# A decode attention kernel: transposes, scores and value product in rounds of 1024 rows, with the evacuation waits moved

## The chip, the cores and the metric

One core of a Trainium2 chip. The calls ran on several chips; the kernel before took a median of 1342.2 to 1343.5 us in every call. The metric is the device time of one execution, in microseconds (us), as the median of several timed runs. Every run told of below was in the fast state; the slow state that programs can fall into did not occur in a run that is used here. A "ratio" is the mean time of one kernel's fast runs over the mean of the other's fast runs of the same rounds, so it is not quite the ratio of the medians that are quoted.

## The reference, cut to what matters

```python
B, Sq, D = 2, 1, 448;  Hq, Hkv, Sk, Dh = 16, 8, 32768, 256      # bf16
q = (x @ wq)                                    # 16 heads, 2 per K/V head
scores = einsum("bhqd,bhkd->bhqk", q, k) * Dh ** -0.5
p = softmax(scores);  a = einsum("bhqk,bhkd->bhqd", p, v) @ wo
out = g * a + (1 - g) * mlp(x)                  # g: a sigmoid gate, small
```

One token a batch row reads all of a K and a V cache of 268 MB each. All else is small. So there are two long jobs: bring 547 MB in, and pass every row of K and V through TensorE.

## The kernel before

The work is cut into 16 groups (batch row × K/V head) of 4 tiles of 8192 rows each, and into units of 512 rows, 1024 in all. A K tile and a V tile are 4 MB each; they land in a ring of five slots. A unit takes three stages on TensorE:

- `T`: 8 transposes of 128x128 blocks of K into a PSUM bank, which ScalarE (even units) or VectorE (odd units) then evacuates to SBUF;
- `B`: scores, 8 matmuls with those blocks as weights (128 columns) and the two query heads of the group moving (2 columns);
- `C`: value product, 4 matmuls with the two heads' probabilities as weights (2 columns) and a row block of V moving (256 columns).

`B` runs 2 units behind `T` (`LB`), `C` 88 units behind (`DU`), because the softmax of a group has to be known first. The last group alone has another form of `C`: V as weights of 128 columns, the probabilities moving.

```python
NB, LB, NKT, NPB = 5, 2, 5, 3          # ring slots, lag of B, SBUF and PSUM buffers of K's transposes
DU = NT * NBL + NBL + NBL // 2         # 88

def T(U):
    wait_landed(E, d, bl)
    if U >= NPB:
        E.wait(evac_eng(U - NPB), ("E", U - NPB))       # bank free again
    for i in range(2 * BR): ... e.transpose(bank[...], kv[:, r, ...], ident_b)

def B(U):
    E.wait(evac_eng(U), ("E", U))                       # this unit evacuated
    ... 8 matmuls, weights buf[:, 128 columns], moving qT_sb (2 columns)

def C(v, bl):
    wait_landed(E, d, bl)
    ... 4 matmuls, weights pt[:, n, :] (2 columns), moving kv[:, r, :] (256 columns)

for U in range(NSTEPU):
    if U < UNITS: T(U)
    if 0 <= U - LB < UNITS: B(U - LB)
    # ... small products of the softmax chain (M1, M2, L, OT), cut ...
    if U >= DU: C((U - DU) // NBL, (U - DU) % NBL)
```

The SP queue issues the loads in the order of need; each waits until TensorE has released the slot.

## Time and profile before

| | before |
|---|---|
| time, median (3 runs) | 1342.33 us |
| span of the profiled run | 1339.0 us |
| TensorE matmul row busy | 98% |
| DMA over the span | 411 GB/s |

The prediction shows and reads the page's busy shares, its chain, the order of instructions and the waits. Three lines of the page (granted TensorE clock, busy share of the 16 DMA engines and GB/s, each in 40 slices) and the loads (count, KB each, us from issue to landing) complete it:

```profile
PEclk9799999999999999999999999999999999999997
DMA  9999999999999999999999999999999999999997
GB/s 394 435 424 431 423 412 420 416 409 417 411 415 413 412 416 410 417 408 409 410 419 412 405 418 410 420 407 414 411 407 417 416 411 413 406 415 416 412 403 301
...
ring<-in_A_k_cache_dram SPq DMA_DIRECT2D x63, 4096.0 KB, 14.6
ring<-in_A_v_cache_dram SPq DMA_DIRECT2D x63, 4096.0 KB, 15.3
```

The DMA row is at 9 up to the last slice, and yet the rate is 423 to 435 in slices 2 to 5 and some 405 to 420 later: an engine counts as busy while a packet is in flight, fast or slow, and from 300 to 1200 us a 32 KB packet took 1.26 us on average (median 1.21).

### The profile page before, as it was taken

What the parts mean: (1) busy time and instruction counts of PE and PEld (TensorE: products, weight loads), DVE (VectorE), ACT (ScalarE), POOL (GpSimd) and SP (SyncE); (2) the same over time, 40 slices, a digit from 0 to 9 for tenths busy, and PEclk for the clock granted to TensorE, in tenths of its full rate; (3) what the DMA queues carried; (4) which work ended last, traced back from release to release, by engine and by line L of the source; (5) the groups of instructions that cost most, each with busy time, mean ns of one, the idle gap of its engine ahead of it and who ended that gap; (6) DMA issues with size and microseconds to landing.
All of it is one profiled execution on the core that took longest, in us unless ns stands there. A gap on an engine that the chain in (4) does not pass through costs nothing.

```text
span 1339.0 us, 44891 instructions
## 1 busy us (share of the span) xinstructions
PE 1309.4 (98%) x21141; PEld 1017.9 (76%) x21141; DVE 387.2 (29%) x641; ACT 538.6 (40%) x597; POOL 1.5 (0%) x10
## 2 busy tenths in 40 slices
PE   4899999999999999999999999999999999999998
PEld 4887777777777777777777777777777777777776
DVE  2342322323223232322322223232232322323220
ACT  2464433434344443343434344343343434444330
POOL 0000000000000000000000000000000000000000
PEclk9799999999999999999999999999999999999997
DMA  9999999999999999999999999999999999999997
GB/s 394 435 424 431 423 412 420 416 409 417 411 415 413 412 416 410 417 408 409 410 419 412 405 418 410 420 407 414 411 407 417 416 411 413 406 415 416 412 403 301
DMA packets 22424, 550.30 MB, mean 411 GB/s; under 512 B 2392, under 2 KB 4576, under 8 KB 4704
## 3 DMA queue, kind: packets, MB, share of 16 engines
q1 hardware_dynamic: 22084, 547.43, 97.8%
q8 instruction: 165, 2.70, 0.7%
q14 instruction: 19, 0.16, 0.0%
q10 hardware_dynamic: 156, 0.01, 0.0%
HBM read 547.43 MB, written 0.00 MB: 409 GB/s over the span
## 4 chain that ended last, share of the span: by engine, by line
PE 96%; DMA 3%; SPq 1%; issue 0%; ACT 0%; DVE 0%
PE psT L374 41%; PE ps_o L448 38%; PE ps_s L393 13%; DMA ring<-in_A_k_cache_dram 3%; PE ps_o L453 1%; PE psT L462 1%; PE ps_m L426 1%; SPq L314 0%; PE ps_m L409 0%; PE ps_m L404 0%; PE ps_o L348 0%; PE ps_o L352 0%; PE ps_o L360 0%; SPq L301 0%; PE ps_m L415 0%
## 5 line engine op out<-in xcount | busy, mean ns | idle before, releaser
L507 ACT COPY KT<-psT 128x1024 bf16<-128x1024 bf16 x512 | 518.3, 1012 | 744.6 <-PE psT L374 744.6
L374 PE MATMUL psT<-ident_b,ring 128*128 128x128 bf16 x8192 | 640.1, 221 | 11.3 <-DMA ring<-in_A_k_cache_dram 9.7
L374 PEld LDWEIGHTS psT<-ident_b,ring 128*128 128x128 bf16 x8192 | 465.3, 98 | 222.6 <-issue 203.1
L509 DVE COPY KT<-psT 128x1024 bf16<-128x1024 bf16 x512 | 354.2, 692 | 901.7 <-PE psT L374 901.6
L448 PE MATMUL ps_o<-ring,PT 128*2 128x256 bf16 x3840 | 570.8, 272 | 0.0
L393 PE MATMUL ps_s<-qT_sb,KT 128*128 128x2 bf16 x8192 | 351.3, 164 | 1.1 <-issue 0.9
L393 PEld LDWEIGHTS ps_s<-qT_sb,KT 128*128 128x128 bf16 x8192 | 313.3, 96 | 1.9 <-issue 1.5
L448 PEld LDWEIGHTS ps_o<-ring,PT 128*2 128x2 bf16 x3840 | 244.6, 82 | 69.0
L537 ACT ACTIVATE PT<-ps_s,negm 128x256 bf16<-128x256 f32 x32 | 16.5, 545 | 0.5
L453 PE MATMUL ps_o<-PT,ring 128*128 128x2 bf16 x512 | 13.8, 164 | 2.1 <-issue 2.1
L453 PEld LDWEIGHTS ps_o<-PT,ring 128*128 128x128 bf16 x512 | 13.5, 100 | 2.8 <-issue 2.8
L340 PE MATMUL ps_m<-xT,ring 128*128 128x2 bf16 x128 | 3.5, 165 | 9.4 <-DMA ring<-in_A_wq_dram 9.4
L598 DVE TENSOR_REDUCE mx<-ps_s 128x2 f32<-128x512 f32 x16 | 10.9, 682 | 1.1 <-PE ps_s L393 1.1
L340 PEld LDWEIGHTS ps_m<-xT,ring 128*128 128x128 bf16 x128 | 3.5, 104 | 9.5 <-issue 9.5
L462 PE MATMUL psT<-ring,attnT 128*2 128x448 bf16 x32 | 9.8, 481 | 0.3 <-DVE attnT L625 0.3
L426 PE MATMUL ps_m<-ident_f,o_sb 2*128 2x2 f32 x60 | 9.4, 258 | 0.3 <-DVE o_sb L621 0.3
L621 DVE TENSOR_SCALAR o_sb<-ps_o,rl 2x256 f32<-2x256 f32 x15 | 7.1, 472 | 6.7 <-PE ps_o L448 6.5
L426 PEld LDWEIGHTS ps_m<-ident_f,o_sb 2*128 2x128 f32 x60 | 8.1, 191 | 0.6 <-DVE o_sb L621 0.4
L462 PEld LDWEIGHTS psT<-ring,attnT 128*2 128x2 bf16 x32 | 3.2, 105 | 5.7 <-issue 4.1
L625 DVE TENSOR_TENSOR attnT<-ps_o,rl 128x2 bf16<-128x2 f32 x2 | 0.2, 159 | 23.3 <-PE ps_o L453 23.3
L404 PE MATMUL ps_m<-ident_f,mx 128*2 128x128 f32 x32 | 6.1, 272 | 0.0
L409 PE MATMUL ps_m<-diag,ones_f 2*128 2x2 f32 x32 | 6.1, 256 | 0.0
(54 smaller groups left out, 61.9 us busy)
## 6 DMA issues: line engine op xcount, KB each, us to landing
ring<-in_A_k_cache_dram SPq DMA_DIRECT2D x63, 4096.0 KB, 14.6
ring<-in_A_v_cache_dram SPq DMA_DIRECT2D x63, 4096.0 KB, 15.3
ring<-in_A_k_cache_dram SPq DMA_DIRECT2D x4, 1024.0 KB, 16.5
ring<-in_A_v_cache_dram SPq DMA_DIRECT2D x4, 1024.0 KB, 17.3
ring<-in_A_wo_dram SPq DMA_DIRECT2D x1, 3584.0 KB, 14.6
ring<-in_A_wq_dram SPq DMA_DIRECT2D x1, 3072.0 KB, 10.2
ring<-in_B_w_dram SPq DMA_DIRECT2D x1, 1568.0 KB, 35.2
ring<-in_B_w_dram SPq DMA_DIRECT2D x1, 1344.0 KB, 30.7
```

What stands on the lines that cost most here:

```text
L340: E.ins(lambda e, w=w, xk=xk, kc=kc, kvh=kvh, j=j, hh=hh: e.matmul(ps_qT[:, kvh, j, hh, :], w, xk, start=(kc == 0), stop=(kc == KC)), key= ...
L374: E.ins(lambda e, bank=bank, i=i, kv=kv, r=r, j=j: e.transpose(bank[:, i * P:(i + 1) * P], kv[:, r, j * P:(j + 1) * P], ident_b[:, :]), ke ...
L393: E.ins(lambda e, pss=pss, n=n, i=i, j=j, buf=buf, kvh=kvh, b=b: e.matmul(pss[:, n, :], buf[:, (2 * i + j) * P:(2 * i + j + 1) * P], qT_sb ...
L426: E.ins(lambda e, j=j: e.matmul(ps_m[:, C_OT + 2 * j:C_OT + 2 * j + 2], o_sb[g % 2][0:2, j:Dh:2], ident_f[0:2, 0:2], start=True, stop=True ...
L448: E.ins(lambda e, g=g, kv=kv, r=r, n=n, pt=pt: e.matmul(ps_o[g % 2][0:2, 0:Dh], pt[:, n, :], kv[:, r, :], start=(n == 0), stop=(n == NT * ...
L453: E.ins(lambda e, g=g, kv=kv, r=r, n=n, j=j, pt=pt: e.matmul(ps_o[g % 2][:, 2 * j:2 * j + 2], kv[:, r, j:Dh:2], pt[:, n, :], start=(n == 0 ...
L462: E.ins(lambda e, c=c, kvh=kvh, hh=hh, j=j: e.matmul(ps_a, attnT[:, kvh, j, hh, :], wo_v[:, h, j * Dm:(j + 1) * Dm], start=(c == 0), stop= ...
L507: E.ins(lambda e: e.copy(buf[:, :], bank[:, :]), key=("E", U))
L509: E.ins(lambda e: e.tensor_copy(buf[:, :], bank[:, :]), key=("E", U))
L537: E.ins(lambda e, hh=hh: e.activation(PT[g % 2][:, :, hh], ps_s[g % 2][:, :, hh], ACTF.Exp, bias=negm[g % 2][:, hh:hh + 1], scale=SCALE, a ...
L598: E.ins(lambda e: e.tensor_reduce(mx[g % 2][:, :], ps_s[g % 2].rearrange("p n h -> p h n"), AX.X, ALU.max), key=("MX", g))
L621: E.ins(lambda e: e.tensor_scalar(o_sb[g % 2][:, :], ps_o[g % 2][0:2, 0:Dh], rl[g % 2][0:2, 0:1], None, op0=ALU.mult), key=("OS", g))
```

## The change

The intent: fewer borders between the stages, and no wait at the head of the transposes and scores, so that their weights could be loaded ahead.

```diff
@@ T @@
-                if U >= NPB:
+                if NPB <= U <= DU + 1:
                     E.wait(evac_eng(U - NPB), ("E", U - NPB))
@@ B @@
-                E.wait(evac_eng(U), ("E", U))
+                if U + LB <= DU + 1:
+                    E.wait(evac_eng(U), ("E", U))
@@ C @@
+            def wait_units(U):
+                for V in (U, U + 1):
+                    if V < UNITS:
+                        E.wait(evac_eng(V - NPB), ("E", V - NPB))
+                for V in (U - LB, U + 1 - LB):
+                    if V < UNITS:
+                        E.wait(evac_eng(V), ("E", V))
+
-            def C(v, bl):
+            def C(v, bl, ahead=None):
 ...
+                    if ahead is not None and i == 2:
+                        wait_units(ahead)
@@ main loop @@
-            for U in range(NSTEPU):
-                if U < UNITS:
-                    T(U)
-                if 0 <= U - LB < UNITS:
-                    B(U - LB)
 ...
-                if U >= DU:
-                    C((U - DU) // NBL, (U - DU) % NBL)
+            for U0 in range(0, NSTEPU, 2):
+                pair = (U0, U0 + 1)
+                for U in pair:
+                    if U < UNITS:
+                        T(U)
+                for U in pair:
+                    if 0 <= U - LB < UNITS:
+                        B(U - LB)
 ... (the small products, for U in pair)
+                for U in pair:
+                    if U >= DU:
+                        C((U - DU) // NBL, (U - DU) % NBL, U0 + 2 if U % 2 else None)
```

## The prediction

> **What bounds the kernel now.** I read the page of the run before first (busy shares, slices, the chain that ended last), then the waits of the engines and of the DMA queue, then the instructions in order of time, then the stretches of the span with their DMA rate.
>
> The page says TensorE:
>
> ```profile
> PE 1309.4 (98%) x21141; PEld 1017.9 (76%) x21141; DVE 387.2 (29%) x641; ACT 538.6 (40%) x597; POOL 1.5 (0%) x10
> ...
> PE psT L374 41%; PE ps_o L448 38%; PE ps_s L393 13%; DMA ring<-in_A_k_cache_dram 3%; PE ps_o L453 1%; PE psT L462 1%; PE ps_m L426 1%; SPq L314 0%; PE ps_m L409 0%; PE ps_m L404 0%; PE ps_o L348 0%; PE ps_o L352 0%; PE ps_o L360 0%; SPq L301 0%; PE ps_m L415 0%
> ```
>
> The chain is TensorE for 96% of the span: transposes of K (L374), value product (L448), scores (L393). The queue's own waits agree: every load of a ring slot waited for TensorE to release the slot, hardly ever the reverse.
>
> ```profile
> SPq L314 <- PE ps_o L448: 618.2, 59, 11.0
> SPq L314 <- PE ps_s L393: 609.3, 64, 17.2
> ```
>
> But a busy matmul row does not mean that work flows. The instructions in order of time, one unit of 512 rows in mid-kernel (columns: start us, length us, engine, line):
>
> ```profile
> 600.43 0.27 PE L448 MATMUL ps_o<-ring,PT 128*2 128x256 bf16 x1
> 600.63 0.45 PEld L374 LDWEIGHTS psT<-ident_b,ring 128*128 128x128 bf16 x8 [0.22 <-issue]
> 600.64 0.62 PE L374 MATMUL psT<-ident_b,ring 128*128 128x128 bf16 x8
> ...
> 601.10 0.34 PE L393 MATMUL ps_s<-qT_sb,KT 128*128 128x2 bf16 x8
> ...
> 601.37 0.60 PE L448 MATMUL ps_o<-ring,PT 128*2 128x256 bf16 x4
> 601.89 0.45 PEld L374 LDWEIGHTS psT<-ident_b,ring 128*128 128x128 bf16 x8 [0.22 <-issue]
> 601.90 0.62 PE L374 MATMUL psT<-ident_b,ring 128*128 128x128 bf16 x8
> ```
>
> First matmul to first matmul: transposes 0.46 us, scores 0.27, value product 0.53: 1.26 us a unit. Now the same transposes and scores before the value product has begun:
>
> ```profile
> 64.22 0.61 PE L374 MATMUL psT<-ident_b,ring 128*128 128x128 bf16 x8
> ...
> 64.67 0.34 PE L393 MATMUL ps_s<-qT_sb,KT 128*128 128x2 bf16 x8
> ...
> 64.87 0.61 PE L374 MATMUL psT<-ident_b,ring 128*128 128x128 bf16 x8
> ```
>
> There they take 0.45 and 0.20. And four value matmuls alone need (0.60 − 0.27)/3 = 0.11 each, 0.43 together. So a unit holds 0.45 + 0.20 + 0.43 = 1.08 us of work and 0.18 us of switching: about 0.07 going into the value product and 0.11 going out of it (0.10 before the weight load of L374 and 0.01 in its first matmul).
>
> **Is that switch a wait on a semaphore, or a cost of the switch itself?** The first transpose carries a wait on an evacuation. Two observations say that the wait is not the cause. In the stretch at 64 us the same transposes carry the same waits, and their weight loads follow the last score matmul without a gap. And late in the kernel a 128-column weight load follows a 2-column product with no semaphore to wait for (the final projection, L462, then the last value product, L453):
>
> ```profile
> 1321.28 1.30 PE L462 MATMUL psT<-ring,attnT 128*2 128x448 bf16 x6
> ...
> 1322.51 0.57 PEld L453 LDWEIGHTS ps_o<-PT,ring 128*128 128x128 bf16 x20 [0.39 <-issue]
> ```
>
> Its last matmul starts at 1322.23 and streams for 0.19 us (448 columns, by the spacing of its neighbours), to 1322.42; the load comes 0.09 us later, the same gap as at 600.54 to 600.63. So the 0.18 us is the price of going from 128-column weights to 2-column weights and back.
>
> **What the Trainium skill says.** "TensorE: Matmul & The Clock Gate", step-by-step section: the engine pulls weight loads ahead of matmuls in flight. The trace agrees within a stage and from transposes to scores, and differs at the border to and from the value product, where nothing is pulled ahead. The same page, section on weight-path modes: fast weight load is on only for weights of 128 columns that are not fp32. L374 and L393 have 128, L448 has 2, so the border is one between two kinds of load; the trace shows the gap, not the mode. "DMA: Bandwidth & Descriptors", Specifications: a fabric ceiling of 435 GB/s. The trace, in the stretch at the start where TensorE waits for K, comes close to it with 428:
>
> ```profile
> 50.00:160.00 110.00, 107.78 (x1903) 91.52 (x1904) 38.55 (x66) 52.72 (x57) 0.00 (x0) 0.94 1.00 428
> 160.00:300.00 140.00, 140.00 (x2209) 107.33 (x2206) 40.57 (x66) 57.56 (x65) 0.00 (x0) 1.00 1.00 414
> 300.00:1290.00 990.00, 990.00 (x15621) 759.90 (x15620) 289.38 (x472) 406.02 (x448) 0.00 (x0) 1.00 0.99 413
> ```
>
> The last three columns are granted clock, DMA busy share, GB/s. After 160 us TensorE alone sets the rate at 413. The busy share is near 1 in both, so it does not show the reserve; the rate does.
>
> **The change part by part.** (1) Two units a round: TTBBCC instead of TBCTBC. Arithmetic, bytes and evacuations are unchanged; one of two switches into and out of the value product goes: 0.18 us a pair. All three stages run together for units 88 to 1023, 936 units or 468 pairs: 468 × 0.18 = 84 us of TensorE time. Before unit 88 and after 1023 there is little to save. (2) The waits leave the transposes and scores; four stand in the value product, ahead of the third matmul of its second unit. At most three become instructions of their own on the sequencer, which runs about a unit ahead; I give them nothing. The last evacuation must be there in time. From the round's start: second transposes are all issued at 0.86 us; the vector copy starts 0.26 us after such an issue (601.04 to 601.30 for the scalar one) and takes 0.69, so it ends near 1.8; the scalar copy, for the first unit, runs 0.66 to 1.68. The waiting matmul is due at 0.90 + 0.40 + 0.09 + 6 × 0.108 = 2.03, its weight load one matmul earlier, 1.92. So the wait is over some 0.1 us before it is needed. (3) Once a group of 64 units the softmax chain on ScalarE (two exponentials of 0.55 + 0.18 us) may delay an evacuation: 0.1 to 0.2 us × 16, under 3 us.
>
> Thus TensorE's unit falls from 1.26 to about 1.17 us. A group now takes 81.77 us (the transposes of the output recur in the chain at 185.73, 267.50, 349.27); 64 × 1.26 = 80.64, so 1.13 goes to the group's small products. TensorE alone would come to 1342 − 84 = 1258.
>
> **But the transfers can't follow.** A K and a V tile are 8.39 MB for 16 units: 16 × 1.17 + 1.13/4 = 19.0 us, 441 GB/s. More than the 428 measured and the skill's 435. So the bound moves to DMA. When TensorE waits for data, two of five ring slots are in use and three are on order, so the queue stays deep, as in the 428 stretch. Floor, as an estimate: the page's 550.30 MB at 428 GB/s are 1286 us; 2 us before the first packets; 7.6 us from the last landing (TensorE resumes at 1331.4) to the end at 1339.0; 3 us for the 16 engines not finishing together (in the 428 stretch the first and last completion of one load lie 3 to 5 us apart). Sum 1299 us of span. The timed median is 3.3 us above the profiled span: **1302 us**, 3.0% faster. Of 84 us about 40 arrive.
>
> **Rivals.** *TensorE keeps the bound, with a new stall in the value product:* if the wait ends late, each round loses it. The margin is only 0.1 us, and TensorE has 0.3 us a tile to give (9.5 against DMA's 9.8), four rounds, so 0.07 us a round, before it is again the slower. A stall of 0.10 us a round leaves 468 × 0.08 = 37 us, 1305; one of 0.14 leaves 19 us, 1323; one over 0.18 is a loss. For it: the close margin. Against it: neither copy has other work in most rounds. *The gap belongs to the wait after all:* then moving the waits would save all switches, 1258 without DMA, but DMA still gives 1302. *No reserve in DMA:* busy share 0.99 already; if saturated transfers average 10.05 us for 4 MB rather than 9.8, about 1325, within 2%. For it: loads of 4 MB landed 10.2 us apart through the steady part, and some packets take longer than usual. Against it: from 50 to 120 us seven loads landed 9.93 us apart, and mid-kernel issue to landing stays near 14.5 us without growing, so the queue runs almost dry there. *Slower* needs a stall of over 0.24 us a round, twice what the margin could be wrong by.
>
> **Range and chances.** DMA at 428 to 432 with little skew gives 1290; a partial stall or a rate of 421 gives 1320. The 2% line is 1315.5. Faster 0.82, within 0.15, slower 0.03.
>
> **What would show it.** Rounds of 2.34 us where data are there: 16 transposes, 16 scores, 8 value matmuls, each with one gap of 0.09. GB/s in the middle rising from 413 to about 426; the wait of transposes or value product for the ring's loads appearing by some 30 to 45 us in total; issue to landing rising from 14.6 to over 20 us; hardly any wait of L448 for an evacuation. It is wrong if TensorE still shows no wait for loads, if idle time stands within the eight value matmuls, or if the rate stays at 413 with deep queues.

## The result, and the profile after

| | before | after |
|---|---|---|
| time, median (4 runs each, same rounds) | 1342.24 us | 1312.27 us |
| ratio of the fast runs | | 0.9779 (0.9762 to 0.9796) |
| span of the profiled run | 1339.0 us | 1310.5 us |
| DMA over the span | 411 GB/s | 420 GB/s |

Faster by 2.2%. The page of the changed kernel, the lines for the engines, the rate and the chain that ended last:

```profile
PE 1232.0 (94%) x21141; PEld 1028.0 (78%) x21141; DVE 388.7 (30%) x641; ACT 538.6 (41%) x597; POOL 1.5 (0%) x10
...
GB/s 394 435 421 423 428 430 429 430 429 428 426 428 430 429 430 428 426 428 429 429 429 416 425 426 427 425 427 422 421 419 423 422 428 418 430 419 421 429 346 295
...
PE 51%; DMA 47%; SPq 1%; issue 0%; DVE 0%
```

The chain was TensorE for 96% before; now DMA holds 47% of it. The rate stays near its early level up to the last two slices. The loads now wait in a deep queue:

```profile
ring<-in_A_k_cache_dram SPq DMA_DIRECT2D x63, 4096.0 KB, 29.8
ring<-in_A_v_cache_dram SPq DMA_DIRECT2D x63, 4096.0 KB, 31.4
```

From issue to landing is twice what it was: with a load landing about every 10 us, about three 4 MB loads are on order. And TensorE now waits for them (columns of the waits: us in total, times, longest):

```profile
PEld psT L374 <- issue: 100.4, 433, 1.7
PEld psT L374 <- DMA ring<-in_A_k_cache_dram: 54.1, 41, 5.7
PE psT L374 <- DMA ring<-in_A_k_cache_dram: 42.3, 34, 5.7
...
PE ps_o L464 <- DMA ring<-in_A_v_cache_dram: 13.9, 2, 13.7
```

"issue" ahead of the transposes' weight loads, the border out of the value product, came 898 times and 203 us before; it is now 433 times and 100 us: half. One round where the data are there:

```profile
601.25 0.90 PEld L374 LDWEIGHTS psT<-ident_b,ring 128*128 128x128 bf16 x16 [0.23 <-issue]
601.25 1.07 PE L374 MATMUL psT<-ident_b,ring 128*128 128x128 bf16 x16
...
602.16 0.54 PE L394 MATMUL ps_s<-qT_sb,KT 128*128 128x2 bf16 x16
...
602.63 1.03 PE L459 MATMUL ps_o<-ring,PT 128*2 128x256 bf16 x8
...
603.59 0.90 PEld L374 LDWEIGHTS psT<-ident_b,ring 128*128 128x128 bf16 x16 [0.22 <-issue]
603.60 1.07 PE L374 MATMUL psT<-ident_b,ring 128*128 128x128 bf16 x16
```

2.35 us for two units instead of 2 × 1.26 = 2.52. The eight value matmuls take 0.97 us to the next transposes, 8 × 0.109 + 0.10: no stall among them, though the waits now stand there. The gap ahead of the transposes is as long as before, though these carry no wait any more.

### The profile page after: what moved, and what is told of

Its sections match the earlier page's. It is cut to its first block, busy times and chain, and to the rows that moved or that the text cites. A ratio compares the mean times of both kernels' runs of the same rounds, so it can differ in the third digit from the quotient of the medians.

```text
span 1310.5 us, 45768 instructions
## 1 busy us (share of the span) xinstructions
PE 1232.0 (94%) x21141; PEld 1028.0 (78%) x21141; DVE 388.7 (30%) x641; ACT 538.6 (41%) x597; POOL 1.5 (0%) x10
## 4 chain that ended last, share of the span: by engine, by line
PE 51%; DMA 47%; SPq 1%; issue 0%; DVE 0%
DMA ring<-in_A_k_cache_dram 45%; PE psT L374 22%; PE ps_o L459 19%; PE ps_s L394 8%; DMA ring<-in_A_v_cache_dram 3%; SPq L314 0%; PE ps_m L427 0%; PE ps_o L348 0%; SPq L301 0%; PE ps_m L410 0%; PE ps_m L405 0%; PE ps_o L352 0%; PE ps_o L360 0%; PE psT L473 0%; PE ps_o L464 0%
## 5 line engine op out<-in xcount | busy, mean ns | idle before, releaser
L374 PE MATMUL psT<-ident_b,ring 128*128 128x128 bf16 x8192 | 553.4, 221 | 45.8 <-DMA ring<-in_A_k_cache_dram 42.3
L459 PE MATMUL ps_o<-ring,PT 128*2 128x256 bf16 x3840 | 497.1, 273 | 0.2
L459 PEld LDWEIGHTS ps_o<-ring,PT 128*2 128x2 bf16 x3840 | 284.5, 83 | 84.6 <-issue 0.6
L394 PE MATMUL ps_s<-qT_sb,KT 128*128 128x2 bf16 x8192 | 278.4, 163 | 0.8 <-issue 0.8
L394 PEld LDWEIGHTS ps_s<-qT_sb,KT 128*128 128x128 bf16 x8192 | 259.6, 96 | 1.0 <-issue 1.0
L464 PE MATMUL ps_o<-PT,ring 128*128 128x2 bf16 x512 | 14.2, 164 | 16.4 <-DMA ring<-in_A_v_cache_dram 13.9
L464 PEld LDWEIGHTS ps_o<-PT,ring 128*128 128x128 bf16 x512 | 13.7, 100 | 17.1 <-DMA ring<-in_A_v_cache_dram 14.0
## 6 DMA issues: line engine op xcount, KB each, us to landing
ring<-in_A_k_cache_dram SPq DMA_DIRECT2D x63, 4096.0 KB, 29.8
ring<-in_A_wo_dram SPq DMA_DIRECT2D x1, 3584.0 KB, 29.8
```

Of the source, the lines that this page charges most:

```text
L374: E.ins(lambda e, bank=bank, i=i, kv=kv, r=r, j=j: e.transpose(bank[:, i * P:(i + 1) * P], kv[:, r, j * P:(j + 1) * P], ident_b[:, :]), ke ...
L394: E.ins(lambda e, pss=pss, n=n, i=i, j=j, buf=buf, kvh=kvh, b=b: e.matmul(pss[:, n, :], buf[:, (2 * i + j) * P:(2 * i + j + 1) * P], qT_sb ...
L459: E.ins(lambda e, g=g, kv=kv, r=r, n=n, pt=pt: e.matmul(ps_o[g % 2][0:2, 0:Dh], pt[:, n, :], kv[:, r, :], start=(n == 0), stop=(n == NT * ...
L464: E.ins(lambda e, g=g, kv=kv, r=r, n=n, j=j, pt=pt: e.matmul(ps_o[g % 2][:, 2 * j:2 * j + 2], kv[:, r, j:Dh:2], pt[:, n, :], start=(n == 0 ...
```

## The experiments

The theory after the result: (1) the border into and out of the value product costs 0.18 us, whatever waits stand there, and pairing saves one of two; (2) that would be worth 80 us, but the loads set the end. Left open by the result: the loads ended 14 us later than I had worked out. All runs of one call share the runs of the kernel before.

### 1. The rounds alone, and the waits alone

`e1_pairs_only` takes the changed kernel and puts the waits back:

```diff
-                if NPB <= U <= DU + 1:
+                if U >= NPB:
...
-                if U + LB <= DU + 1:
-                    E.wait(evac_eng(U), ("E", U))
+                E.wait(evac_eng(U), ("E", U))
...
-  C(..., U0 + 2 if U % 2 else None)
+  C(...)
```

> The rounds of two units, with the waits left at the head of the transposes and of the scores, as before. Theory (the gain is one switch a pair, and the loads are then the bound): same as the changed kernel, 1312 +/- 3 us, DMA about 420 GB/s over the span, the gap ahead of the transposes still 0.09 us, once a pair. Rival (the wait at the head keeps weights from being loaded ahead, so the moved waits are part of the gain): TensorE keeps more gaps and the time lies between, 1318 to 1335 us.

Measured: 1312.17 us, ratio to before 0.9773 (0.9759 to 0.9788), correct. The same as the whole change. Its timeline:

```profile
600.61 0.90 PEld L374 LDWEIGHTS psT<-ident_b,ring 128*128 128x128 bf16 x16 [0.23 <-issue]
```

`e2_waits_only` takes the kernel before, with units one by one, and moves the waits for the next unit ahead of the third value matmul:

```diff
+            def wait_unit(U):
+                if U < UNITS: E.wait(evac_eng(U - NPB), ("E", U - NPB))
+                if U - LB < UNITS: E.wait(evac_eng(U - LB), ("E", U - LB))
...
+                    if ahead is not None and i == 2: wait_unit(ahead)
...
-                    C((U - DU) // NBL, (U - DU) % NBL)
+                    C((U - DU) // NBL, (U - DU) % NBL, U + 1)
```

(with the waits in `T` and `B` dropped as in the change)

> The order of before (one unit a round), with the waits for the next unit's evacuations moved into the value product ahead of its third matmul. Theory (a done wait costs nothing, the gap belongs to the change between 2-column and 128-column weights): same as before, 1342 +/- 3 us, unit 1.26 us, gap ahead of the transposes still 0.09 us. Rival (the wait causes the gap): the gap of 0.09 to 0.10 us at the head of the transposes goes in 936 units, so TensorE is faster by up to 85 us and the time falls to the loads' floor, about 1312 us.

Measured: 1346.64 us, ratio 1.0028 (1.0017 to 1.0039), correct. In its timeline, the gap is there without a wait:

```profile
601.31 0.45 PEld L374 LDWEIGHTS psT<-ident_b,ring 128*128 128x128 bf16 x8 [0.23 <-issue]
```

What follows: all of the gain is the order; the moved waits give nothing in either order, and alone cost about 4 us. (In the order of rounds both kernels end at the loads' floor, so their times alone could not show it. Before the loads bind, the first three groups take 76.12 us in both.) In the instruction records the first transpose starts 205 ns after the last value matmul in all three (before, with the waits moved, and after), so the gap is not the wait's. Where the 4 us arise I did not settle: seven of 13 groups still take 81.77 to 81.79 us, the others up to 0.9 us more, which is 2.9 us in all; the moved waits also bring 877 more instructions (45768 against 44891).

### 2. Less work for TensorE

`e3_before_light` and `e3_after_light` stream half of V's columns in the value product. They compute a wrong result on purpose, and load everything.

```diff
-  ps_o[g % 2][0:2, 0:Dh], pt[:, n, :], kv[:, r, :],
+  ps_o[g % 2][0:2, 0:(Dh if n == 0 else P)], pt[:, n, :], kv[:, r, 0:(Dh if n == 0 else P)],
```

> Wrong result on purpose. The order and the waits of before, as many instructions, but value matmuls stream 128 columns of V instead of 256 (the very first of a group still 256). TensorE's unit falls by about 4 x 0.054 = 0.21 us to 1.05 us, all bytes are still loaded. Theory (the changed kernel stands at the floor of the loads): about the time of the changed kernel, 1312 +/- 4 us, though the order is that of before and TensorE has 130 us less to do. Rival (the changed kernel is still bound by TensorE): well below 1312, down to 1270 us.

> Wrong result on purpose. The changed kernel with value matmuls of 128 columns instead of 256, same number of instructions and bytes. Theory (floor of the loads): 1312 +/- 3 us, no gain, TensorE's waits for loads grow by about 100 to 190 us in total. Rival (TensorE or its stalls still bound part of the run): 1270 to 1300 us.

Measured: 1312.17 and 1312.62 us, ratios 0.9774 (0.9757 to 0.979) and 0.9779 (0.9764 to 0.9793); both outputs wrong, as meant. From 300 to 1200 us (the last three columns are granted clock, DMA share, GB/s), first the order of before, then that of after:

```profile
300.00:1200.00 900.00, 820.05 (x14602) 708.64 (x14601) 269.79 (x443) 379.00 (x422) 0.00 (x0) 0.93 1.00 425
```

```profile
300.00:1200.00 900.00, 794.84 (x14570) 690.35 (x14568) 271.15 (x442) 378.92 (x422) 0.00 (x0) 0.94 1.00 425
```

Four kernels (after, e1 and these two) with different orders and loads on TensorE meet at 1312 us. It is a floor that TensorE does not set, and even the old order reaches it when TensorE has less to do. (TensorE's waits for loads grew by less than the 100 to 190 us expected: from 56 us in the changed kernel to 120 in `e3_after_light`.)

These two runs also settle a rival that the theory left open: that the gap comes from the 256 moving columns of the value product, and not from its weights. With 128 moving columns, as many as a transpose has, value matmuls start 55 ns apart, and the first transpose 149 to 152 ns after the last one (medians of the two runs). With 256 it was 108 and 205. So some 95 ns beyond the spacing are left either way.

### 3. Less to load

`e4_before_half` and `e4_after_half` load only the first half of the rows of each tile and use these twice, so that TensorE's work is unchanged. The result is wrong on purpose.

```diff
-                    parts = [(view(d), src)]
+                    parts = [(view(d)[:, 0:SLOT // 2], src[:, 0:SLOT // 2])]
...  (in T and both forms of C)
-  kv[:, r, ...]
+  kv[:, r % (R // 2), ...]
```

> Wrong result on purpose. Order and waits of before; K and V loads fetch only the first half of each tile's rows (2 MB instead of 4; the first K and the last V tile stay whole), and the matmuls read those rows twice, so TensorE, ScalarE and VectorE do the same instructions. The loads need about 285 MB, 670 us, and can't bind in the middle. Theory: TensorE's own time; the middle keeps 1.26 us a unit and 81.8 us a group; only the waits for loads at the start and the end go, about 30 us: 1310 us +/- 10.

> Wrong result on purpose. The changed kernel with the same halved loads. Theory (a switch into and out of the value product costs 0.18 us and one of two goes): 468 pairs x 0.18 = 84 us below the halved kernel of before, so about 1226 us +/- 10, pair 2.34 us, group about 76 us. Rival (the switch saved is dearer or cheaper than that, or the wait in the value product stalls): difference under 60 or over 100 us.

Measured: 1325.72 and 1244.67 us, both outputs wrong, as meant. The difference, 81.05 us, is what the order saves on TensorE when data are always there. The transposes of a group's output recur every 81.77 us in the first and every 76.12 us in the second: 5.65 us a group of 32 pairs, 0.177 us a pair. (I had both totals some 16 to 19 us too low, outside my ±10: I took 30 us off for the waits for loads, and the first value product started only 11.5 us earlier than in the kernel before, 91.7 against 103.2. The difference is not touched.)

```profile
300.00:1200.00 900.00, 900.00 (x14206) 691.23 (x14203) 262.89 (x429) 368.88 (x408) 0.00 (x0) 1.00 0.55 207
```

```profile
300.00:1200.00 900.00, 900.00 (x15250) 748.65 (x15247) 283.09 (x460) 396.64 (x439) 0.00 (x0) 1.00 0.59 223
```

TensorE never idles in either, and does 7% more matmuls in the same 900 us (15250 against 14206).

### 4. Why the floor is 1312 and not 1302

The packet records of the changed kernel show when engines end. A 32 KB packet takes 1.21 us, so the 8 packets that an engine has in a 4 MB load take 9.7. Yet from 200 to 1246 us the loads completed 9.97 us apart, and the first and the last of a load's 16 completions lay 15 us apart on average (2.5 in the kernel before). At the end 16 packets were in flight at 1297 us and exactly 8 from 1299 to 1303. So half of the engines run behind.

What is special about them? The queue of instruction fetches has 169 packets of 16 KB. Such a packet takes about 1.05 us, and the load's packet behind it 1.70 instead of 1.21: 1.53 us lost to that engine. Following the packets of each engine end to start, the fetches fall, as far as this can be told, on 8 of the 16. The trace does not number the engines, so this is an inference. Then 169 / 8 × 1.53 = 32 us lie on each of those 8, not the 16 of an even share.

The spacing bears this out. From 200 to 1246 us the changed kernel's loads took, in sum, 27.2 us more than 8 × 1.213 us each; its 138 fetches there give 26.4 us on each of 8 engines, and 13.2 in an even share. In e1 and the two runs of part 2 the same sums are 26.3 and 26.0, 24.8 and 25.6, 27.2 and 26.2.

`e5_fewer_instr` tests it: half of the transposes and scores are left out, which takes away 16384 of TensorE's instructions and no byte of K or V.

```diff
-                for i in range(2 * BR):
-                    r, j = bl * BR + i // 2, i % 2
+                for i in range(BR):
+                    r, j = bl * BR + i, 0
...  (in B, j = 0 alone; evacuations of 512 columns instead of 1024)
```

> Wrong result on purpose. The changed kernel with half of the transposes and half of the scores left out (head columns 128 to 255): 16384 of TensorE's instructions fewer (of 45768 in all), the same bytes of K and V. TensorE is then far from being the bound. Question: why the loads end 14 us later than bytes over 428 GB/s said. Theory A (half of the 16 DMA engines also carry the instruction fetches, 169 packets of 16 KB, each costing about 1.5 us there, about 21 on each of 8 engines; those 8 end last): about 60 fetches fewer, 7.6 fewer on each of the 8, 11 us earlier: 1301 +/- 3 us, and the first and last engine finish closer together. Theory B (the floor is a matter of the bytes of K and V and of memory alone): unchanged, 1312 +/- 2 us.

Measured: 1300.05 us, ratio to before 0.9684 (0.967 to 0.9699). It was found correct within the tolerance, though it computes less than the reference: it is no version to use. The line of the fetch queue (packets, MB, share), first of the changed kernel, then of this run:

```profile
q8 instruction: 169, 2.77, 0.8%
```

```profile
q8 instruction: 105, 1.72, 0.5%
```

64 fetches fewer, 8 on each of 8 engines, 8 × 1.53 = 12.2 us as estimated; measured 1312.27 − 1300.05 = 12.2 us, across two calls (12.8 by the two ratios to before). The loads completed 9.87 us apart instead of 9.97, and the spread fell from 15 to 12.2 us. From 200 to 1246 us 16.0 us went beyond the bare packets, and 85 fetches give 16.3. Less work on TensorE can't be the reason, since the two runs of part 2 had that too and gained nothing. The run also halves the evacuations, which no run does alone; but the packets got no faster (median 1.21 us in both). An even share over 16 engines would have given half of it, 6 us.

### 5. Attempts to use it, all failed

If 8 engines are late, bytes should go to the other 8. A transfer of 8 partitions runs on 8 engines (Trainium skill, "DMA: Bandwidth & Descriptors", the part on how many engines a transfer takes). The trace agrees: 8 to 10 packets were in flight while wo alone moved (1292 to 1312 us). `e6_rebalance` cuts w2 and wo into 16 such transfers:

```diff
+                if kind in ("W12", "WO"):
+                    o, src = parts.pop()
+                    w = P // CUT                                  # CUT = 16
+                    parts += [(o[c * w:(c + 1) * w], src[c * w:(c + 1) * w]) for c in range(CUT)]
```

> Right result. The changed kernel with the loads of w2 and wo (1.6 and 3.7 MB) cut into 16 transfers of 8 partitions each, which should run on 8 of the 16 DMA engines instead of on all. Moves about 0.33 MB, 12 us of one engine at 27 GB/s, from one half of the engines to the other. Theory A (the end is set by the 8 engines that carry the instruction fetches): 1300 +/- 4 us if the transfers fall on the other 8, 1324 +/- 4 us if they fall on the same 8. Theory B (engines share alike and the end is set by the total): within 3 us of 1312.

Measured: 1366.59 us, ratio 1.0179 (1.0158 to 1.02), correct: none of the forecasts. wo's packets ran from 1263.6 us on, while the two V loads issued ahead of it landed in full only at 1281.1 and 1290.9; the first of their completions had come at 1254.2 and 1263.9. So the 8 engines that took wo look to be those that had done their part of the V loads: the early ones, as wanted. But a packet of wo took 154 ns (median) instead of 74, and wo needed 70 us. In `e7_wo_eight` (wo alone) and `e8_wo_w2_eight` (with w2) the 8 partitions of a transfer lie 16 apart:

```diff
-  parts += [(o[c * w:(c + 1) * w], src[c * w:(c + 1) * w]) for c in range(CUT)]
+  parts += [(o[c:P:CUT], src[c:P:CUT]) for c in range(CUT)]
```

> Right result. Like the run that cut w2 and wo, but wo alone, and each of its 16 transfers takes 8 partitions that lie 16 apart instead of side by side. In that run the 8 engines that took wo were those that had finished the earlier loads first, so not those with the instruction fetches, but its packets took 152 ns instead of 74 and 70 us went there. Theory A (the 8 engines with the fetches set the end, and side by side partitions slowed the packets): packets near 74 ns again; 3.67 MB / 16 = 0.23 MB leave each slow engine, 8.5 us: 1304 +/- 3 us. Rival B (small transfers on 8 engines are slow in themselves): wo again takes about 70 us, 1340 us or more. Rival C (the end isn't set by those 8 engines): 1312 +/- 2 us with packets near 74 ns.

> Right result. As the run with wo alone, with w2 (1.57 MB) on the 8 engines too. Theory A: 0.33 MB or 12 us leave each slow engine: 1300 +/- 3 us, and the first and the last engine end within 4 us or so. Rival B: over 1340 us. Rival C: 1312 +/- 2 us.

Measured: 1341.37 us, ratio 0.9993 (0.9985 to 1.0001), and 1357.59 us, ratio 1.0113 (1.0097 to 1.013), both correct. wo's packets took 144 ns, so spreading its partitions cured nothing: rival B. There is a second cost that the texts on record did not foresee. In e7 the SP queue issued five parts of wo within 3 us and the other eleven only from 1267.0 to 1285.7 us, some 2 us apart, so the V load behind them went out at 1286.9 us instead of 1254.1, and from 1272 to 1288 us only 8 or 9 packets were in flight. What held the issues back is not shown. `e9_shift_rows` moves one packet of each late engine in 9 V tiles, with packets of 32 KB:

```diff
+                    if d in SHIFTED:                              # every 7th V tile
+                        parts = [(view(d)[a:b:s], src[a:b:s])
+                                 for a, b, s in ((0, 112, 1), (112, P, 2), (113, P, 2))]
```

> Right result. The changed kernel; in 9 of the 64 V tiles the load is cut in three: partitions 0 to 111 on all 16 engines (7 packets of 32 KB each instead of 8) and the last 16 partitions as two transfers of 8 partitions on 8 engines, which earlier runs showed to be those without instruction fetches. Theory A (the 8 engines with the fetches set the end): they carry 9 packets less, 9 x 1.21 = 11 us: 1302 +/- 4 us if the small transfers cost the other 8 little beyond their bytes; if each small transfer costs them 2 us more, they become the bound and little is left: 1308 to 1314. Theory B (all engines alike): 1312 or more.

Measured: 1546.56 us, ratio 1.1504 (1.147 to 1.1537), correct: neither theory. The rate falls at each of those tiles:

```profile
GB/s 403 425 430 330 369 428 424 303 329 430 427 307 266 425 427 368 212 390 415 417 261 318 407 422 297 287 364 422 384 247 336 411 428 269 275 399 425 273 204 301
```

After the first such load (issued at 133 us) most packets of 32 KB take 2.2 to 2.5 us instead of 1.21, and the last of the three parts landed 32 us after its issue (up to 63 us in the later ones). The page's section on the descriptor swizzle says that in a transfer to 128 partitions each engine writes one port of SBUF. That with 112 or 8 partitions engines and ports no longer match is my inference from it; no run here isolates that. e6 to e8 fit the account of which engines are early, but none of the four tests what a better balance would give.

### 6. The border removed in another way

`e10_no_switch` is the kernel before with the last group's form of the value product for all groups, so that all stages load weights of 128 columns:

```diff
-    GS = NG - 1
+    GS = 0
...
-                        E.wait("dve", ("OS", g - 2))
+                        E.wait("dve", ("O", g - 2))
```

> Right result. The kernel before, order and waits as they were, but the value product of every group in the form that only the last group had: rows of V as 128-column weights, two columns of probabilities moving. So all three stages load weights of 128 columns. Theory (the gap belongs to the change between 2-column and 128-column weights): no gap of 0.09 us in the order of before, unit 0.45 + 0.20 + 0.20 = 0.85 us, and the loads bind. There are some 7700 instructions more, so about 29 more fetches of 16 KB, 3.6 more on each of 8 engines at 1.5 us: 1312 + 5 = 1317 +/- 3 us. Rival (order or waits make the gap): gap stays, unit 0.95 us or more. Rival on the floor (fetches don't matter): 1312 +/- 2 us.

Measured: 1355.60 us, ratio 1.0105 (1.0089 to 1.0121), correct. The time expected is missed by 39 us, yet the gap is gone:

```profile
602.21 0.35 PE L453 MATMUL ps_o<-PT,ring 128*128 128x2 bf16 x8
602.40 0.77 PEld L374 LDWEIGHTS psT<-ident_b,ring 128*128 128x128 bf16 x8
602.42 1.01 PE L374 MATMUL psT<-ident_b,ring 128*128 128x128 bf16 x8
...
603.23 0.40 PE L393 MATMUL ps_s<-qT_sb,KT 128*128 128x2 bf16 x8
```

The transposes start 0.21 us after the eight value matmuls begin, which is what eight matmuls at 25 to 27 ns take. So order and waits are those of before, and with one kind of weights there is no border: the second pillar of the theory. (The moving columns changed too, from 256 to 2; part 2 shows that the gap does not hang on their number.) But the transposes now take 0.81 us instead of 0.46. The page's line for the granted clock says why:

```profile
PEclk9697565555556555575665555555565565555556
```

Half clock for most of the run (mean 0.567; 0.98 before), with the busy row at 96%. What lowered it is not shown. Short matmuls beside the transposes are not enough: in this same run, from 80 to 100 us, transposes and 2-column scores with hardly anything else ran at 1.00. The clock fell when the 2-column value product joined them (0.83 from 100 to 110 us, 0.54 from 300 to 1200). This run therefore says nothing on the floor of the loads.

## Why the prediction was right or wrong

**The bound before and the price of the border** held. The measured pair saves 0.177 us where 0.18 was worked out, and 81 us in total where 84 was (e4). That a satisfied wait is free and the border itself costs was argued from two places of the old trace; e1, e2 and e10 show it, together with the value products of 128 columns (e3).

**The waits in the value product** cost nothing there, as put: no stall among the eight matmuls. Nor did they bring anything (e1).

**The loads become the bound**: shown by e3 and by the waits and landing times of the profile after. The rate in mid-run was to be about 426; it is 425 to 429. (The line that gave 428 has TensorE busy for 107.78 of 110 us, so it hardly waited for K there. But the queue was deep, as supposed: the loads landed 17 to 44 us after their issue.) Waits for loads were to be 30 to 45 us in total; they are 56, above the range: 42.3 for K and 13.9 for V, of which 13.7 is one wait near the end. Issue to landing was to pass 20 us; it is 29.8.

**The size of the floor** was the term that was off. The predicted 1302 lay 10 us below 1312.27. The sum's term "3 us for the 16 engines not finishing together" was mis-sized: it came from the spread in the early stretch, as if it stayed there. The spread grew to 15 us on average, because, by the account of part 4, the instruction fetches burden only half of the engines: by subtraction the term should have been 17 (1305.2 − 2 − 1286). I used one mean rate (550.30 MB at 428 GB/s), which spreads the fetches over all 16. The last load landed at 1305.2 us by the trace, where my terms (2 + 1286 + 3) say 1291: 14 us late. Two small terms went the other way: 5.3 us from that landing to the end instead of 7.6, and 1.8 us between the span and the timed median instead of 3.3. 14 − 2.3 − 1.5 = 10. That the total was off by 10 us and not by 14 is luck. The range of 1290 to 1320 covered it, and faster by over 2% came true, with 2.2% where 3.0% was put.

**Of the rivals**, a stall in the value product did not occur, and the gap was not the wait's. The third, no reserve in DMA, came true in part: from 10.20 us between loads (before) the spacing fell to 9.97, where I had 9.8 and the rival 10.05. Its sum was wrong as well: 128 loads of 0.25 us more are 32 us on top of 1302, so 1334 and not 1325.

No run beats the changed kernel with the whole computation; e1 equals it with fewer instructions and is the simpler of the two.

## What to carry to other kernels

Read the cost of a border between stages from start-to-start times, once with the neighbour stage and once without it, and look for the same border without a wait before blaming a wait. When an engine's gain runs into the loads, work out the floor for the most burdened DMA engine, instruction fetches included, and not from the mean rate. Where long matmuls are replaced by many short ones, look at the granted clock as well: here it fell to 0.567 (e10), for a reason not shown.

## What the Trainium skill lacked or had wrong

- "TensorE: Matmul & The Clock Gate" (step-by-step section) has weight loads pulled ahead of running matmuls. It lacks that this fails between weights of 2 and of 128 columns: 205 ns from the last value matmul to the first transpose where the stream needs 108, with or without a wait (149 to 152 where it needs 55, e3), and 0.177 us for a way in and out.
- The same page (Part 4) says that full clock does not engage for transposes and gives some 275 ns each. In the kernel before, among scores and value products, one takes 221 ns and they start 56 ns apart, at a granted clock of 1.00. When the clock drops stays open: with all other matmuls at 2 columns its mean was 0.567 (e10), but 1.00 in a stretch of that run with hardly more than transposes and scores (80 to 100 us).
- "Runtime: NRT & Kernel Launch" (instruction fetch mechanics) calls the cost of crossing a 16 KiB boundary mostly hidden. With DMA as the bound it isn't: 64 fetches of 16 KB fewer gave 12.2 us (e5). No page says that the fetches fall on half of the engines, as these runs suggest.
- "DMA: Bandwidth & Descriptors" (rules for kernel authors) advises 128 partitions. Neither it nor another page has what less did to the packets here: 1792 bytes took 144 to 154 ns instead of 74 in transfers of 8 partitions (e6, e7), and 32 KB of the loads after one cut into 112, 8 and 8 partitions took mostly 2.2 to 2.5 us instead of 1.21 (e9).
